# RWKV attention and two MoE layers: most tiles' keys and outputs are turned through DRAM, and the second MoE's row fetches change places with its weights

## The chip, the cores and the metric

One core of one Trainium2 chip runs the kernel. The metric is device time in microseconds (us). Before the change, three runs took 840.63, 841.93 and 843.02 us, a median of 841.93.

## The reference

Three layers follow one another, in fp32. B = 4 batches, H = 8 heads, S = 768 steps, D = 48.

```python
for t in range(S):                               # attention, state is 48 x 48 per head
    cur = einsum('bhd,bhe->bhde', u[None] * k[t], v[t])
    y[t] = einsum('bhd,bhde->bhe', r[t], state + cur)
    state = w[t][..., None] * state + einsum('bhd,bhe->bhde', k[t], v[t])
x = y as (B*S = 3072 tokens, H*D = 384)
xn = x / sqrt(mean(x*x) + 1e-6) * rms_g          # MoE 1: gated, 384 -> 1536 -> 384
x = (silu(xn @ w_gate) * (xn @ w_val)) @ w_out
e = argmax(x @ w_gate2)                          # MoE 2: the best of 8 experts, 384 -> 1024 -> 384
out = prob[e] * sigmoid(x @ w_output_gate)[e] * (relu(x @ w1[e]) @ w2[e])
```

## The kernel before

**Attention in tiles.** The recurrence is worked in 24 tiles, each of 128 steps of one batch (six chunks of four batches). A tile is a generator, `attention` (L384), in steps that end at each `yield`. In each step of 128 tokens the keys and receptances are scaled by running products of the decay. A tile's 8 heads lie as four pairs (`NPR`): `kq`, the scaled keys, is 128 partitions (channels of a pair) by 4 x 128 tokens. The steps are: the backward scan (L404, VectorE); `kq` (L422); the forward scan `rq`, its product and the bonus reduction (L430, L433, L440); the decay of the state; the scores on TensorE and their masking to `am` (L530, L538, VectorE); the turning of `kq` into tokens x channels (`kt`: four TensorE transposes, L469, and a copy by ACT, L471; they precede the scores); the values (L563) and key times value (`sp`, L552), the sum `y` (L572), its mean square (ACT, POOL); the state's update (L588); the scaling of `y` (L596, ACT); and the turning of `y` into channels x tokens (three TensorE transposes, L600), from which `xh` (ACT, L604) and `xl` (VectorE, L607) are split: each product of MoE 1 and MoE 2 is three passes, high x high, high x low, low x high (`mm3`, all at L191).

The last chunk's four tiles (20 to 23) need no `kt`, because no state follows.

**MoE 1 in stages.** Eight stages, j = 0 to 7, hold 384 tokens (three tiles) each. TensorE works first-layer products (`l1`, two halves a block f: gate and value) and second-layer ones (`l2`) for 12 blocks f; ACT makes `sil`, VectorE the product (`sil`, L670), ACT `hh` (L672), VectorE `hl` (L675). In stage j the attention of the three tiles of stage j + 1 is worked between them.

**Who sets the order.** Each engine runs its own queue in program order. `Plan` (L772) is a table of slots: a stage has one slot after the first half of `l1`, one after `hh` and one after `l2`, 36 in all, and a tile's step number k is written at slot a * TGAP + OFFS[k], for its tile a = 0, 1, 2 of the stage. Before, TGAP is 9 and OFFS is (0, 2, 4, 6, 8, 10, 11, 13, 15). SP's queue issues nearly all DMAs, in program order; a DMA whose source is not ready holds those behind it.

**MoE 2 in units.** Rows of each expert were scattered to DRAM (`scr`). Unit 0 is 256 rows of the largest expert, unit 1 its other 272; units 2 to 8 are experts 1 to 7, 448 to 352 rows. A unit is `l1` in KF2 = 8 blocks f (plus two for `l2`); in it the next unit's rows are turned (`turn_next`, L759) and split, and the next expert's weights are fetched (`raw`, L178 and L165; three 384 KB buffers in flight in MoE 1's last stages, four later), and split by ACT (L160) and VectorE (L161). The rows of a unit are fetched by `gather` (four DMAs into `z`, L751, and one into `xg`, L1095). Before, unit 0 fetches unit 1's rows at f = 2, loads the ids of all seven other experts to SP at f = 4 (L1406), and fetches unit 2's rows at f = 6; expert 1's weights come in unit 1, and unit 1 fetches unit 3's rows at f = 5.

Of the kernel before, what the change touches and what calls it, by code (L numbers as in the profile page):

```python
# [9 lines left out]
F32 = mybir.dt.float32  # L10
# [12 lines left out]
def kernel(  # L23
# [17 lines left out]
    TURN_AT=2,  # L41
# [15 lines left out]
    DSLOT=(1, 2),  # L57
    OFF0=((0, 2.0, 6.2, 8.5, 8.5, 11.0, 12.5, 12.5, 15.2), (9.4, 11.9, 14.1, 16.9, 17.2, 19.9, 19.9, 21.8, 23.3), (17.8, 19.3, 24.0, 26.0, 26.8, 27.8, 30.3, 30.8, 30.8)),
    OFFS=(0, 2, 4, 6, 8, 10, 11, 13, 15),
    TGAP=9.0,  # L60
    START_SEQ=(-1, -6, -3, -6, 99, -12, 0, 0, -6, 0, 1, 1, 0, -1, 0, 1, -6, 1, 0, 9, -5, 0, 2, 1, 0, 9, 2, -1, 0, -5, 1, 2, 1, 9, 1, -7, 2, 2, 9, 2, 9, -2, 1, 2, 2, 9, -6, -6, -1, 2),
):
    nc = tc.nc
# [4 lines left out]
    P = 128  # L68
# [311 lines left out]
            )  # L380

    START = START_SEQ

    def attention(c, i, xh, xl, col):  # L384

# [34 lines left out]
        front = c["front"].rearrange("p (a t) -> p a t", t=SEG)  # L420
        nc.vector.reciprocal(front[:, :, 0:1], decay)
        nc.vector.tensor_tensor(out=kq, in0=kT, in1=kq, op=ALU.mult)  # L422
        kt_mul = nc.vector if i in KT_DVE else nc.gpsimd
        if bare and i not in KT_DVE:
            kt_mul.tensor_tensor(out=kT, in0=kT, in1=rT, op=ALU.mult)
# [172 lines left out]
        xT = bank("m", 3, [P, KD, P])  # L598
        for kk in range(KD):
            nc.tensor.transpose(xT[:, kk], y2[:, kk * P:(kk + 1) * P], c["ident"])  # L600
        cs = slice(col, col + P)
        for kk in range(KD):
            gk = c["g"][:, kk:kk + 1]
# [198 lines left out]
    with tc.manual_schedule():  # L802
# [184 lines left out]
        for j in range(NB):  # L987
# [24 lines left out]
            for f in range(KF + 2):  # L1012
                if f < KF:
                    if j == 0:
                        weights_to(f + f // 2 + 1)
                    hs[f] = l1(f, xs[0], xs[1], n, slot, j == 0 and f // 2 < WHOLE)
                if f >= 2:
                    if (f - 2) // 2 in routed:
                        exhaust(routed.pop((f - 2) // 2))
                    if j == 0 and (f - 2) // 2 < WHOLE:  # L1020
                        l2_whole(f - 2, hs.pop(f - 2), acc)
                    else:
                        if (f - 2) // 2 not in wo:
                            split_wo((f - 2) // 2)
                        l2(f - 2, hs.pop(f - 2), acc)
                    slot()
                if j == NB - 1:
                    if f == 3:
                        lead = pick(c)
                        xw = expert_weights(0, lead)  # L1030
                    if f >= 4:
                        next(xw, None)
                    if f == KF - 3:
                        both = ring_view([2, EARLY * KD])
                        z0 = both[:, 0].rearrange("p (j c) -> p j c", c=DQ)
                        xT0 = both[:, 1].rearrange("p (k t) -> p k t", k=KD)
                        early = scr.rearrange("(e a) c -> e a c", e=E)[ds(lead, 1)]
                        load_blocks(z0, early, 0, EARLY // 32)
                        xg0 = late.tile([P, EARLY // P, ROW - DM], F32, name="xg0")
                        nc.sync.dma_start(  # L1040
                            out=xg0,
                            in_=early[:, 0:EARLY, DM:ROW].rearrange("o (t p) c -> p (o t) c", p=P),
                        )
                    if f == KF:
                        x0 = ring_view([2, KD, EARLY], FR)
                        for kk in range(KD):
                            turn(z0, xT0, kk)
                        for kk in range(KD):
                            split_in(xT0, EARLY, x0[:, 0], x0[:, 1], kk)
                if j == 1:  # L1050
                    for e in INIT_AT.get(f, ()):
                        init_rows(c, e)
            plan.finish()
            if j == 0:
                decs.close()
                late = ctx.enter_context(
                    tc.tile_pool(name="late", bufs=1, side="right", reuse_waits="tile")
                )
                route_constants(c, late)
                pr = ph1.enter_context(tc.tile_pool(name="pr", bufs=1, reuse_waits="tile"))  # L1060
            if j == NB - 2:
                rawp = ph1.enter_context(tc.tile_pool(name="rawp", bufs=3, reuse_waits="tile"))
            if j + 1 < NB:
                xr = pr.tile([P, nt, WIDTH], F32, tag="xr", name="xr")
# [252 lines left out]
        xg_cur, x_cur = xg0, (x0[:, 0], x0[:, 1])  # L1317
        for ui, (k, r0, n) in enumerate(units):
            last_of = ui + 1 == NU or units[ui + 1][0] != k
            if ui and last_of:  # L1320
                nxw = expert_weights(k + 1, expert[k + 1]) if k + 1 < E else iter(())
            xh, xl = x_cur
            a, b2 = ew[k]
# [9 lines left out]
            if ui == 0:  # L1333
                plan.add(
                    route(c, starts[NB - 1], sizes[NB - 1], xr, True), 0,
                    ROUTE_AT,
                )

            def gather_unit(i):
# [20 lines left out]
            for f in range(KF2 + 2):  # L1360
                if f < KF2:
# [13 lines left out]
                if ui and f == GATHER_AT and ui + 2 < NU:  # L1375
                    gathered[ui + 2] = gather_unit(ui + 2)
                if ui + 1 < NU:
                    if ui and f >= TURN_AT:
                        next(turns, None)
                    if not ui and f == KF2:  # L1380
                        exhaust(turns)
# [16 lines left out]
                    plan.step()  # L1398
                if ui == 0 and f == 2:
                    gathered[1] = gather_unit(1)  # L1400
                if ui == 0 and f == KF2 - 2:
                    gathered[2] = gather_unit(2)
                if ui == 0 and f == 4:
                    ids = order()
                    expert += [
                        nc.values_load(  # L1406
                            ids[0:1, q:q + 1], engines=(mybir.EngineType.SP,), min_val=0,
                            max_val=E - 1,
                        )
                        for q in range(E - 1)  # L1410
                    ]
            exhaust(post)
            if by_row:
                for i, o in enumerate(acc):
# [78 lines left out]
```

## Time and profile before

| | |
|---|---|
| median of three runs | 841.93 us |
| profiled execution | 841.91 us, span 840.2 us |
| TensorE (PE) busy | 811.9 us, 97% |
| weight loads (PEld) | 763.7 us, 91% |
| VectorE (DVE) | 536.5 us, 64% |
| ScalarE (ACT) | 327.3 us, 39% |
| GpSimd (POOL) | 199.5 us, 24% |
| TensorE clock granted, mean | 0.99 of full speed |
| DMA | 88.97 MB, 106 GB/s over the span |

Idle time that the profile names "idle before" is that of the engine of the row, and the arrow names what ended it. A timeline row with x3 is three like instructions joined, and its duration runs from the first start to the last end; TensorE's matmuls overlap, so that what one costs is read from the next one's start, not from its duration.

### The profile page before, as it was taken

The numbers are of one execution on the slowest core, as the hardware profiler recorded it, in microseconds if no ns is written. First come the engines' busy times: TensorE is split into PE (matmuls) and PEld (weight loads), VectorE is DVE, ScalarE is ACT, GpSimd is POOL, SyncE is SP. The second block draws the span as 40 slices with busy tenths as digits, with TensorE's granted clock in tenths as the row PEclk, the third lists the DMA queues.
The fourth block names the chain that finished last, engine by engine and source line by source line (L and its number), as shares of the span: only waits on it lengthen the run. The fifth ranks groups of instructions, "written<-read, shape, count | busy, mean of one in ns | idle before, by whom it ended". The sixth has DMA issues, their size and how long they took to land. (4 is left out here: it accounts for less than half of the span.)

```text
span 840.2 us, 19796 instructions
## 1 busy us (share of the span) xinstructions
PE 811.9 (97%) x8007; PEld 763.7 (91%) x8007; DVE 536.5 (64%) x1155; ACT 327.3 (39%) x718; POOL 199.5 (24%) x286
## 2 busy tenths in 40 slices
PE   8799999999999999999999999999979999999995
PEld 5588789999999999999999999999879999999994
DVE  8788857755774774685575476334747686677751
ACT  6756543233323233223323322323425434454430
POOL 4544523213321231132131131010101022112111
PEclk9899999999999999999999999999999999999998
DMA  8955527561320240222122020023167655565410
GB/s 214 286 162 161 151 59 211 139 150 48 104 70 11 58 121 24 55 90 58 48 87 68 25 81 2 2 86 95 54 165 189 170 124 159 155 177 154 153 44 24
DMA packets 78500, 88.97 MB, mean 106 GB/s; under 512 B 23345, under 2 KB 69847, under 8 KB 78407
## 3 DMA queue, kind: packets, MB, share of 16 engines
q1 hardware_dynamic: 74768, 78.10, 34.6%
q0 software_dynamic: 3312, 9.56, 3.1%
q8 instruction: 63, 1.03, 0.5%
q14 instruction: 31, 0.25, 0.1%
q10 hardware_dynamic: 326, 0.03, 0.0%
HBM read 71.25 MB, written 16.78 MB: 105 GB/s over the span
## 5 line engine op out<-in xcount | busy, mean ns | idle before, releaser
L191 PE MATMUL a<-xh,gv 128*128 128x384 f32 x1152 | 317.8, 342 | 1.4 <-ACT xh L604 1.4
L191 PEld LDWEIGHTS a<-xh,gv 128*128 128x128 f32 x1152 | 210.8, 188 | 4.0 <-ACT xh L604 1.6
L191 PE MATMUL a<-xl,gv 128*128 128x384 f32 x576 | 194.3, 337 | 0.5 <-DVE xl L607 0.5
L191 PE MATMUL l<-wo,hh 128*128 128x400 f32 x504 | 134.6, 348 | 0.0
L670 DVE TENSOR_TENSOR sil<-a,sil 128x384 f32<-128x384 f32 x84 | 46.7, 556 | 108.3 <-PE a L191 106.5
L191 PE MATMUL a<-xh,w1s 128*128 128x272 f32 (+7 forms) x384 | 107.9, 342 | 4.5 <-DVE hl L1142 4.5
L191 PEld LDWEIGHTS a<-xl,gv 128*128 128x128 f32 x576 | 108.6, 189 | 1.2 <-DVE xl L607 0.7
L663 ACT ACTIVATE sil<-a 128x384 f32<-128x384 f32 x96 | 47.2, 492 | 156.1 <-PE a L191 155.6
L672 ACT ACTIVATE hh<-sil 128x384 fp32r<-128x384 f32 x84 | 44.1, 525 | 133.3 <-DVE sil L670 133.3
L191 PEld LDWEIGHTS l<-wo,hh 128*128 128x128 f32 x504 | 90.8, 188 | 1.0
L191 PE MATMUL l<-wo,hl 128*128 128x400 f32 x252 | 86.5, 343 | 0.0
L278 POOL DMA_INDIRECT out_dram<-row,iu x30 | 35.3, 1178 | 188.9 <-DVE row L1153 164.7
L1142 DVE SCALAR_TENSOR_TENSOR hl<-a,hh 128x256 fp32r<-128x256 f32 (+8 forms) x72 | 38.6, 539 | 62.6 <-ACT hh L1141 62.4
L191 PEld LDWEIGHTS a<-xh,w1s 128*128 128x128 f32 x384 | 71.3, 192 | 5.9 <-DVE hl L1142 4.7
L675 DVE TENSOR_TENSOR hl<-sil,hh 128x384 fp32r<-128x384 f32 x84 | 55.7, 663 | 30.2 <-ACT hh L672 29.6
L1141 ACT ACTIVATE hh<-a 128x256 fp32r<-128x256 f32 (+8 forms) x72 | 34.3, 476 | 98.1 <-PE a L191 96.4
L191 PE MATMUL l<-hh,rows 128*128 128x272 f32 (+4 forms) x240 | 67.9, 347 | 0.0
L191 PE MATMUL a<-xl,w1s 128*128 128x272 f32 (+7 forms) x192 | 65.5, 341 | 0.2 <-DVE xl L764 0.2
L191 PEld LDWEIGHTS l<-wo,hl 128*128 128x128 f32 x252 | 47.2, 188 | 0.0
L191 PEld LDWEIGHTS l<-hh,rows 128*128 128x128 f32 x240 | 44.6, 191 | 1.0
L191 PE MATMUL l<-rows,hh 128*128 128x384 f32 (+2 forms) x176 | 45.2, 338 | 0.0
L453 POOL TENSOR_TENSOR y<-vt,g 128x384 f32<-128x384 f32 x18 | 15.1, 837 | 123.5 <-issue 85.8
(259 smaller groups left out, 1335.3 us busy)
## 6 DMA issues: line engine op xcount, KB each, us to landing
raw<-in_moe_w_dram SPq DMA_DIRECT2D x64, 384.0 KB, 3.9
set<-in_feat_dram SPq DMA_DIRECT2D x46, 192.0 KB, 3.7
rk<-in_rkv_dram SPq DMA_DIRECT2D x19, 384.0 KB, 4.1
scr<-zrow SPq DMA_DIRECT2D x8, 788.0 KB, 7.3
set<-in_feat_dram SPq DMA_DIRECT2D x46, 96.0 KB, 2.5
vt<-in_rkv_dram SPq DMA_DIRECT2D x23, 192.0 KB, 3.1
raw<-in_moe_w_gate_dram SPq DMA_DIRECT2D x8, 384.0 KB, 4.7
raw<-in_moe_w_val_dram SPq DMA_DIRECT2D x8, 384.0 KB, 5.8
```

Of the source, the lines that this page charges most:

```text
L191: nc.tensor.matmul(o, a, b, start=start and i == 0, stop=stop and i == 2, skip_group_check=True)
L278: ins = nc.gpsimd.indirect_dma_start(out=dst, out_offset=bass.IndirectOffsetOnAxis(ap=idx, axis=0), in_=rows, in_offset=None, bounds_check ...
L453: nc.gpsimd.tensor_tensor(out=y, in0=vv, in1=g.unsqueeze(2).to_broadcast([P, H, D]), op=ALU.mult)
L663: nc.scalar.activation(out=sil, in_=o, func=AF.Silu)
L670: nc.vector.tensor_tensor(out=sil, in0=pg[1], in1=sil, op=ALU.mult)
L672: nc.scalar.activation(out=hh, in_=sil, func=AF.Copy)
L675: nc.vector.tensor_tensor(out=hl, in0=sil, in1=hh.bitcast(F32), op=ALU.subtract)
L1141: nc.scalar.activation(out=hh, in_=o, func=AF.Relu)
L1142: nc.vector.scalar_tensor_tensor(out=hl, in0=o, scalar=0.0, in1=hh.bitcast(F32), op0=ALU.max, op1=ALU.subtract)
```

## The change

From tile 9 on (`BLOCKS`), `kq` (except in the last chunk: 11 tiles) and the scaled `y` (15 tiles) are written to a scratch in DRAM by one DMA, and read back by four, each for 32 partitions in pieces of 32 x 4 bytes, so that each 32 x 32 square lands in the place that it has in the turned matrix. One VectorE instruction then turns every square (L567 and L626 of after). The 89 TensorE transposes (44 and 45) and ACT's copies to `kt` of these tiles go. `xh` and `xl` read the turned `y` from SBUF. The tiles of these stages get other slots.

```diff
+    OFFB=(0, 0, 1, 3, 10, 11, 12, 13, 14, 19),
+    TGAPB=8.0,
+    BLOCKS=9,
...
+    def through(place, t, how, z):
+        nc.sync.dma_start(out=place, in_=t)
+        src = place.rearrange(how, i=4, j=4, r=32, c=32)
+        a = z.shape[1] // P
+        for i in range(4):
+            q = z[32 * i:32 * i + 32].rearrange("p (a j c) -> p a j c", a=a, j=4)
+            nc.sync.dma_start(out=q, in_=src[i])
...
+        by_blocks = i >= BLOCKS
+        if not last and by_blocks:
+            kt_z = blk.tile([P, NPR * P], F32, tag="kz", name="kz")
+            through(kd[i % 2], kq, "(j r) a (i c) -> i r a j c", kt_z)
...
-        if not last:
+        if not last and not by_blocks:
             kt_ps = bank("m", 3, [P, NPR, P])
...
+        if by_blocks:
+            if not last:
+                kt = p1.tile([P, NPR, P], F32, tag="kt", name="kt")
+                nc.vector.transpose(out=kt.rearrange("p a t -> p (a t)"), in_=kt_z)
+            yield
...
         nc.scalar.activation(out=y2, in_=y2, func=AF.Copy, scale=ss)
+        if by_blocks:
+            y_z = blk.tile([P, DM], F32, tag="yz", name="yz")
+            through(yd[i % 2], y2, "(j r) (k i c) -> i r k j c", y_z)
+        yield
+        if by_blocks:
+            xT = blk.tile([P, KD, P], F32, tag="yt", name="yt")
+            nc.vector.transpose(out=xT.rearrange("p k t -> p (k t)"), in_=y_z)
...
-                        a * TGAP if j else 0, OFFS if j else OFF0[a],
+                        a * (TGAPB if j > 1 else TGAP) if j else 0,
+                        OFFB if j > 1 else OFFS if j else OFF0[a],
...
-                    if f == KF:
+                    if f == KF - 1:
                         x0 = ring_view([2, KD, EARLY], FR)
...
-            if ui and last_of:
+            if ui > 1 and last_of:
                 nxw = expert_weights(k + 1, expert[k + 1]) if k + 1 < E else iter(())
...
-                next(nxw, None)
+                if ui or f in (KF2 - 2, KF2 - 1):
+                    next(nxw, None)
...
+                if ui == 1 and f == 2:
+                    gathered[2] = gather_unit(2)
+                if ui == 1 and f == KF2 + 1:
+                    next_expert()
+                if ui == 2 and f == 0:
+                    gathered[3] = gather_unit(3)
...
-                    if ui and f >= TURN_AT:
+                    if ui > 1 and f >= TURN_AT + (2 if ui == 2 else 0) or ui == 1 and f >= TURN_AT + 3:
                         next(turns, None)
...
-                if ui == 0 and f == KF2 - 2:
-                    gathered[2] = gather_unit(2)
                 if ui == 0 and f == 4:
                     ids = order()
-                    expert += [
...
+                    next_expert()
+                    nxw = expert_weights(1, expert[1])
```

(`next_expert` loads one id to SP's registers; the next ids are loaded just before each later unit's gather.) Of TensorE's queue only the transposes and the places of the attention's steps change; VectorE's and SP's queues show the rest.

VectorE before, in a stage, from a tile's forward scan (`rq`) to its scores' masks (`am`); `xl` between them belongs to the tile ahead of it, and `sil` and `hl` to MoE 1:

```order
L430 SCALAR_TENSOR_TENSOR rq<-set_81,front 128x516
L433 TENSOR_TENSOR rq<-set_81,rq 128x4x128
L440 TENSOR_REDUCE g<-rk 128x8
L670 TENSOR_TENSOR sil<-a,sil 128x384
L675 TENSOR_TENSOR hl<-sil,hh 128x384
L607 SCALAR_TENSOR_TENSOR xl<-m,g_col,xh 128x128 x3
L490 TENSOR_TENSOR states<-states,kq 128x192
L670 TENSOR_TENSOR sil<-a,sil 128x384
L530 TENSOR_TENSOR am_84<-a,tri_83 128x4x64
L538 TENSOR_TENSOR am_84<-a,tri_83 64x2x64 x2
L530 TENSOR_TENSOR am_85<-m,tri_83 128x4x64
L538 TENSOR_TENSOR am_85<-m,tri_83 64x2x64 x2
```

VectorE now, at the like place in a stage from j = 2 on; the scan is the third tile's, `am` and `kt` are the second tile's, `yt` and `xl` the first tile's:

```order
L448 SCALAR_TENSOR_TENSOR rq<-set_81,front 128x516
L451 TENSOR_TENSOR rq<-set_81,rq 128x4x128
L458 TENSOR_REDUCE g<-rk 128x8
L705 TENSOR_TENSOR hl<-sil,hh 128x384
L548 TENSOR_TENSOR am_84<-a,tri_83 128x4x64
L556 TENSOR_TENSOR am_84<-a,tri_83 64x2x64 x2
L548 TENSOR_TENSOR am_85<-m,tri_83 128x4x64
L556 TENSOR_TENSOR am_85<-m,tri_83 64x2x64 x2
L626 STREAM_TRANSPOSE yt<-yz 128x384
L637 SCALAR_TENSOR_TENSOR xl<-yt,g_col,xh 128x128 x3
L567 STREAM_TRANSPOSE kt<-kz 128x512
```

The third tile's scan now stands ahead of the second tile's masks, and between these and the turning of the second tile's keys (L567, which its key times value needs) lie the first tile's `yt` and `xl`.

SP before, in MoE 2's unit 0, from the last fetch for unit 1 (`xg`, 16 x 10) through the ids of the experts to the fetch of unit 2's rows (`z`, 14 pieces) and expert 1's first weights (`raw`):

```order
L1100 DMA xg<-scr 16x10
L1406 TENSOR_LOAD order
L1406 ISA x2
...
L751 DMA z<-scr 32x14x96
...
L1095 DMA xg<-scr 128x4x10
L178 DMA raw<-in_moe_w_dram 128x3x256
L165 DMA raw<-in_moe_w_dram 128x2x384
```

SP now, at the like place:

```order
L1134 DMA xg<-scr 16x10
L1376 TENSOR_LOAD order
L1376 ISA x2
L181 DMA raw<-in_moe_w_dram 128x3x256
L168 DMA raw<-in_moe_w_dram 128x2x384
...
L181 DMA raw<-in_moe_w_dram 128x3x256
L781 DMA z<-scr 32x14x96
...
L1129 DMA xg<-scr 128x4x10
L168 DMA raw<-in_moe_w_dram 128x2x384
```

One id is loaded in place of seven, and five weight fetches now stand ahead of unit 2's rows.

## Rows read from the trace of the kernel before

**Rows 1.** Windows: microseconds; busy (instructions) per engine; clock; DMA share; GB/s

```profile
334.70:402.90 68.20, 68.20 (x831) 65.85 (x830) 43.09 (x100) 21.71 (x52) 16.15 (x24) 1.00 0.23 63
```

**Rows 2.** Timeline of PE: start, microseconds, line, operation, tile; stage j=3

```profile
361.89 0.52 PE L191 MATMUL l<-wo,hh 128*128 128x400 f32 x2
...
363.52 0.49 PE L600 MATMUL m<-ident,y 128*128 128x128 f32 x3
363.84 0.60 PE L469 MATMUL m<-ident,kq 128*128 128x128 f32 x4
364.20 0.42 PE L191 MATMUL a<-xh,gv 128*128 128x384 f32 x1
364.46 0.34 PE L191 MATMUL a<-xl,gv 128*128 128x384 f32 x1
...
367.23 0.34 PE L191 MATMUL a<-xh,gv 128*128 128x384 f32 x1
...
368.78 0.63 PE L191 MATMUL l<-wo,hh 128*128 128x400 f32 x2
```

**Rows 3.** Timeline of PE: values, key times value, stage j=2

```profile
321.86 0.38 PE L563 MATMUL m<-vt,am 128*32 128x48 f32 x16
...
322.56 0.52 PE L552 MATMUL m<-vt,kt 128*32 128x48 f32 x32
```

**Rows 4.** VectorE by form: count, busy, mean ns, idle before

```profile
L759 DVE STREAM_TRANSPOSE xT<-z 128x384 f32<-128x384 f32 x6 | 4.1, 687 | 0.0
L607 DVE SCALAR_TENSOR_TENSOR xl<-m,g_col,xh 128x128 fp32r<-128x128 f32 x72 | 20.8, 345 | 16.7 <-ACT xh L604 16.6
```

**Rows 5.** Timeline of VectorE: one tile among stage j=3

```profile
360.89 1.22 DVE L430 TENSOR_TENSOR_SCAN rq<-set,front 128x516 f32<-128x516 f32 x1
...
363.26 0.54 DVE L670 TENSOR_TENSOR sil<-a,sil 128x384 f32<-128x384 f32 x1
...
368.47 0.42 DVE L530 TENSOR_TENSOR am<-a,tri 128x256 f32<-128x256 f32 x1 [0.23 <-PE m L523]
...
370.39 0.56 DVE L675 TENSOR_TENSOR hl<-sil,hh 128x384 fp32r<-128x384 f32 x1
```

**Rows 6.** DMA issues: tile, queue, count, KB each, median landing time

```profile
vt<-in_rkv_dram SPq DMA_DIRECT2D x23, 192.0 KB, 3.1
z<-scr SPq DMA_DIRECT2D x8, 168.0 KB, 5.3
...
xg<-scr SPq DMA_DIRECT2D x3, 15.0 KB, 2.0
```

**Rows 7.** Timeline of ACT: end of stage j=2

```profile
325.54 0.53 ACT L672 ACTIVATE hh<-sil 128x384 fp32r<-128x384 f32 x1 [1.18 <-DVE sil L670]
...
328.46 0.61 ACT L596 ACTIVATE y<-y,ss 128x384 f32<-128x384 f32 x1
```

**Rows 8.** Timeline of PE: first matmul of stage j=3

```profile
334.66 0.33 PE L191 MATMUL a<-xh,gv 128*128 128x384 f32 x1
```

**Rows 9.** Windows: ends of MoE1 and of the first expert

```profile
594.00:596.00 2.00, 0.99 (x5) 0.47 (x4) 2.00 (x6) 1.34 (x4) 0.00 (x0) 1.00 0.00 0
627.83:633.83 6.00, 6.00 (x27) 6.00 (x28) 5.40 (x17) 1.80 (x5) 0.00 (x0) 0.52 0.97 218
634.00:636.00 2.00, 2.00 (x18) 2.00 (x17) 2.00 (x4) 1.60 (x3) 0.00 (x0) 1.00 0.89 122
```

**Rows 10.** Timeline of ACT: first expert

```profile
617.75 0.40 ACT L1141 ACTIVATE hh<-a 128x272 fp32r<-128x272 f32 x1 [0.90 <-PE a L191]
624.93 0.84 ACT L160 ACTIVATE w1s<-raw 128x768 fp32r<-128x768 f32 x1 [6.78 <-DMA raw<-in_moe_w_dram]
```

**Rows 11.** Timeline of PE: the first matmul after the wait

```profile
627.83 0.59 PE L191 MATMUL a<-xh,w1s 128*128 128x272 f32 x1 [4.48 <-DVE hl L1142]
```

**Rows 12.** SP queue: start, issue time, transfer

```profile
610.57 0.33 SPq L1100 DMA_DIRECT2D xg<-scr  x1
615.14 1.90 SPq L751 DMA_DIRECT2D z<-scr  x4
```

More of the change, by code (lines that the diff above doesn't have):

```diff
@@ L382 @@
     START = START_SEQ
+    kd = [dram.tile([P, NPR, P], F32, name=f"kd{i}") for i in range(2)]
+    yd = [dram.tile([P, DM], F32, name=f"yd{i}") for i in range(2)]
+    def through(place, t, how, z):
[5 more added lines that the diff above has]
+            nc.sync.dma_start(out=q, in_=src[i])
     def attention(c, i, xh, xl, col):
@@ L596, in attention @@
         nc.scalar.activation(out=y2, in_=y2, func=AF.Copy, scale=ss)
+        if by_blocks:
+            y_z = blk.tile([P, DM], F32, tag="yz", name="yz")
+            through(yd[i % 2], y2, "(j r) (k i c) -> i r k j c", y_z)
         yield
-        xT = bank("m", 3, [P, KD, P])
-        for kk in range(KD):
-            nc.tensor.transpose(xT[:, kk], y2[:, kk * P:(kk + 1) * P], c["ident"])
+        if by_blocks:
+            xT = blk.tile([P, KD, P], F32, tag="yt", name="yt")
+            nc.vector.transpose(out=xT.rearrange("p k t -> p (k t)"), in_=y_z)
+        else:
+            xT = bank("m", 3, [P, KD, P])
+            for kk in range(KD):
+                nc.tensor.transpose(xT[:, kk], y2[:, kk * P:(kk + 1) * P], c["ident"])
         cs = slice(col, col + P)
@@ L1060 @@
                 pr = ph1.enter_context(tc.tile_pool(name="pr", bufs=1, reuse_waits="tile"))
+                blks = ph1.enter_context(ExitStack())
+                blk = blks.enter_context(tc.tile_pool(name="blk", bufs=2, reuse_waits="tile"))
             if j == NB - 2:
+                blks.close()
                 rawp = ph1.enter_context(tc.tile_pool(name="rawp", bufs=3, reuse_waits="tile"))
@@ L1336, with next_expert @@
                     ROUTE_AT,
+                )
+            def next_expert():
+                q = len(expert) - 1
+                expert.append(
+                    nc.values_load(
+                        ids[0:1, q:q + 1], engines=(mybir.EngineType.SP,), min_val=0,
+                        max_val=E - 1,
+                    )
                 )
@@ L1371 @@
                         next(post, None)
-                next(nxw, None)
+                if ui or f in (KF2 - 2, KF2 - 1):
+                    next(nxw, None)
                 if ui >= 3:
                     next(listing, None)
-                if ui and f == GATHER_AT and ui + 2 < NU:
+                if ui == 1 and f == 2:
[4 more added lines that the diff above has]
+                    gathered[3] = gather_unit(3)
+                if ui > 1 and f == GATHER_AT and ui + 2 < NU:
+                    next_expert()
                     gathered[ui + 2] = gather_unit(ui + 2)
                 if ui + 1 < NU:
-                    if ui and f >= TURN_AT:
+                    if ui > 1 and f >= TURN_AT + (2 if ui == 2 else 0) or ui == 1 and f >= TURN_AT + 3:
                         next(turns, None)
@@ L1400 @@
                     gathered[1] = gather_unit(1)
-                if ui == 0 and f == KF2 - 2:
-                    gathered[2] = gather_unit(2)
                 if ui == 0 and f == 4:
                     ids = order()
-                    expert += [
[L1406 to L1411, printed above, removed]
+                    next_expert()
+                    nxw = expert_weights(1, expert[1])
             exhaust(post)
```

## Prediction

> **What bounds the kernel now.** I read the page's busy shares first, then the slices, then windows of single stages, then TensorE's idle time by what ended it. TensorE bounds MoE 1: in stage j = 3, 68.20 us long, it is busy for all 68.20, at clock 1.00, while VectorE works 43.09, ACT 21.71 and DMA has a share of 0.23 [rows 1]. So work taken from TensorE there is worth its full length, and work added elsewhere costs only where TensorE comes to wait for it. Outside the stages TensorE idles in two places that the change touches: between 594 and 596 us it works 0.99 of 2.00 [rows 9], and in the first expert of MoE 2 one matmul stands behind 4.48 us of idle time [rows 11], after which the granted clock is 0.52 for six microseconds [rows 9].
>
> **Transposes that go.** Three of y and four of kq stand between an l2 and an l1: the first starts at 363.52, the first l1 matmul behind them at 364.20, 0.68 later; that matmul's successor comes 0.26 later instead of the usual 0.17 [rows 2]. I charge the extra 0.085 to them: 0.765 us for seven, 0.109 each. Eighty-nine go: 9.7 us. By stage: 21 of them in j = 2, 3 and 4 (2.3 us each), 17 in j = 5 (1.85; tile 20 has no kt), 9 in j = 6 (0.98). ACT loses its copies to kt as well, which were hidden.
>
> **New work on VectorE.** The trace has this square-wise turning for 128x384: 0.687 us [rows 4]. In proportion 128x512 takes 0.92. A stage gets 3 x (0.69 + 0.92) = 4.8 us more; 43.1 + 4.8 is far under 68.2, so VectorE doesn't become the bound. But it works in order, and the new order puts the third tile's scan, product and reduction, the second tile's masks and the first tile's yt and xl ahead of the second tile's kt, for which its key times value waits two slots behind the scores. I walk both queues from the end of the l1 half before the scores. VectorE: sil 0.48, the scan and what follows it 2.37 (360.89 to 363.26), hl 0.5, masks 1.92 (368.47 to 370.39) [rows 5], yt 0.69, ACT's xh 0.35 (as one xl), three xl 0.9 [rows 4], kt 0.92: 8.1 us. TensorE: l2 1.63 (361.89 to 363.52), scores with the old state's part 1.38 (to 368.78), two l1 halves of 1.56 (nine spacings of 0.17) [rows 2], values 0.70 [rows 3]: 6.8. TensorE waits 1.3 us. For the third tile, counted from the end of the scores: VectorE 1.6 (to the masks' end, 368.78 to 370.39) + 0.5 + 0.69 + 0.35 + 0.9 + 0.92 = 5.0, TensorE 1.63 + 1.56 + 0.70 = 3.9: 1.1 us. The first has no such neighbours: 0.1. So 2.5 us a stage come back in j = 2 to 4, 1.4 in j = 5 and none in j = 6. From below the wait may be nothing, if sil or the masks start earlier than in the walk; from above, one more hl (0.5) ahead of each makes 3.5.
>
> **The way through DRAM.** No row shows a write and four reads of 128-byte pieces. For the write I take 2.7 us, between xg's 2.0 and vt's 3.1 (192 KB, as y is); for the issues of the second to fourth read 1.4 (four z issues take 1.90 [rows 12]); for the last read's landing 2.2, near xg's 2.0 (15 KB in pieces of 40 bytes) and under z's 5.3 (168 KB each) [rows 6]. That makes r = 6.3 us; the ends are 5.5 (2.0 + 1.4 + 2.0) and 9.8 (3.1 + 1.4 + 5.3). Keys have ten slots for it, and hide it. The first two tiles' y has five slots (some 9.5 us). The third tile's y has to reach the next stage's first matmul. In stage j = 2, hh of block 10 ends at 326.07 and the scaling, now a slot earlier, takes 0.61 [rows 7]: 326.7. With r, yt 0.69, xh and the first xl 0.35 each the operands are there at 334.4, and that matmul starts at 334.66 before [rows 8], less some 0.3 that the stage has been shortened: a wait of about 0.1 to 0.4, taken 0.4, at each of five boundaries (into j = 3 to 7). There every us that r is above 6.3 costs 5 us in all; beyond some 7.2 the yt of the earlier tiles also holds up VectorE's queue ahead of kt, for 4 us more per us (one in each of j = 2 to 5). SP gets five issues a transfer and waits for the write in between; behind it stand vt and sets for later tiles, which are fetched a tile (some 15 us) ahead, so I cost that at nothing; without this lead a late vt would stop the values.
>
> The Trainium skill, page "DMA: Bandwidth & Descriptors", section "Specifications", gives 512 bytes as the least transfer for line rate, and a read-modify-write below it. That speaks against these 128-byte pieces. The nearest row, xg's 384 pieces of 40 bytes in 2.0 us [rows 6], does not show it; it holds 15 KB where a square read holds 48 or 64.
>
> **Sum of MoE 1.** j = 2 to 4: 3 x (-2.3 + 2.5 + 0.4) = 1.8; j = 5: -1.85 + 1.4 + 0.4 = -0.05; j = 6: -0.98 + 0.4 = -0.6. Together +1.2 us: what the transposes give, VectorE's waits take back.
>
> **MoE 2.** In the 4.48 us, TensorE waits for hl, hl for hh on ACT, and ACT stands in order behind a weight split whose raw landed only at 624.93, 6.78 us after ACT's last work [rows 10]. SP explains the lateness: between the last small fetch (610.57 + 0.33) and the next one (615.14) it loads seven ids, 4.2 us, and then issues unit 2's rows ahead of the first weight [rows 12]. Now one id is loaded (a seventh of 4.2, 0.6) and the first weight leaves near 611.6, where before it stood behind fetches that began at 615.14 and took two more us to issue; so it lands before ACT comes to its split. The stall goes: -4.5. With no idle time ahead of it I let the clock stay up: the six us at 0.52 hold 27 matmuls, where two us at full clock hold 18 of the same kind or near it, so up to 3.0 us; since the counts mix sizes I take 2.3. What is late next is unit 2's rows: the fifth weight waits for a free buffer, that is for the first one's landing (four to six us after 611.6) and split, until some 617.8, so z leaves at 618.3 to 621 and lands near 624 to 625, for turns that start with f = 5 of unit 1; the last split, now behind the copies of the outputs, costs 0.5 at the next boundary (0 to 1.1). The earlier turn for unit 0 takes the 1.0 us of 594 to 596. Sum: -4.5 - 2.3 - 1.0 + 0.5 = -7.3.
>
> Together +1.2 - 7.3 = -6.1. The profiled execution took 841.91 us (span 840.2), as the median of 841.93; **835.8 us**.
>
> **Rivals.**
> (1) The squares come late. For it: four reads of small pieces each behind a write, and z's 5.3 us. Against: xg. At r = 8.1 it costs 1.8 x 5 + 0.9 x 4 = 12.6 more: 848.4 us. It decides for slower (above 844.4) from r = 7.7.
> (2) VectorE's waits don't show and the stages' ends neither, since VectorE idles a third of each stage and slots can drift: all 9.7 us count, and 841.9 - 9.7 - 7.3 = 824.9.
> (3) MoE 2's stall moves instead of going: unit 2's rows, behind five weights and a buffer's release, come as late as the weights did, and TensorE waits at unit 2 with the low clock behind it. For it: the DMA share there was 0.97 [rows 9]. Then only the 1.0 remains: 841.9 + 1.2 - 1.0 = 842.1.
>
> **How the numbers follow.** Forecast 0.48, with a range of its own of 831 to 840 (waits of 1 to 3.5 a stage, the clock's part 1 to 3); late squares 0.22; no waits 0.13; moved stall 0.17. A measurement can tell 0.3%, 2.5 us, from no change: faster is under 839.4, slower over 844.4. The forecast gives 0.44 of faster and 0.04 of same, no waits 0.13 of faster, the moved stall 0.16 of same and 0.01 of slower, late squares 0.02 of same and 0.20 of slower: faster 0.57, same 0.22, slower 0.21. The range of 827 to 846 leaves out most of the late squares, whose upper end (r = 9.8) would be near 864, and half of "no waits".
>
> **What would show it.** Stages j = 2 to 4 of about 68 us, with TensorE waits for kt on VectorE of 1.1 to 1.3 us ahead of key times value, some seven in all, and under 0.5 us for xl or xh at each stage's start; squares that return in about 6 us from the scaling's end; in the first expert no idle time of TensorE over 1 us and a clock of 1.00. Wrong: waits of over 1.5 us at the stages' starts (rival 1), stages of 66 us (rival 2), a wait of several us for z or its turn at unit 2 (rival 3).

## The result

The changed kernel takes 845.89 us (median of six, 843.94 to 848.09) against 841.45 us before: a ratio of 1.0057, with a 95% interval from 1.0038 to 1.0077. It is slower; 835.8 us was forecast. From one trace to the other, stages 2 to 6 of MoE 1 went from 338.5 to 346.6 us (+8.1; forecast +1.2), and MoE 2's first three units with the stage ahead of them from 133.5 to 128.4 (-5.1; forecast -7.3). Three single executions of 1086 to 2781 us, one of them of the kernel before, are left out of the ratios in this document.

Stages are counted here as the code counts them, j = 0 to 7. The rows, and the prediction where it reads them, give two stages of the trace before as j = 2 and j = 3 that are 3 and 4 by this count (the window of [rows 1] is stage 4). The prediction's sum goes by the right count and does not change.

Two windows of the changed kernel: stage j = 4 and a stretch in stage 3 (columns as in [rows 1]; the engines are PE, PEld, DVE, ACT and POOL).

```profile
340.22:410.26 70.04, 66.88 (x810) 64.10 (x810) 46.64 (x106) 19.90 (x49) 17.99 (x24) 1.00 0.40 100
327.58:330.99 3.41, 3.41 (x12) 3.40 (x12) 0.52 (x2) 0.63 (x3) 2.52 (x3) 0.50 0.23 62
```

Where TensorE was busy for the whole of a stage, it now idles 3.2 of 70.04 us, with 21 fewer matmuls. What it waited for in stages 2 to 5 (us in total, times, longest), in the changed kernel:

```profile
PE m L575 <- DVE kt L567: 6.8, 7, 1.8
PE m L575 <- DVE t L766: 3.7, 4, 0.9
PE m L758 <- DVE am L556: 1.7, 3, 0.7
PE a L194 <- DVE am L556: 0.8, 1, 0.8
```

Eleven waits stand ahead of key times value, four ahead of the routing's ranks and an l1 product; there was none of these before. Idle time is not all of it. TensorE's timeline at the first tile of stage 4:

```profile
363.21 0.19 PE L758 MATMUL m<-oh,tri 128*128 128x24 bf16 x1 [0.70 <-DVE am L556]
...
363.93 0.35 PE L586 MATMUL m<-turned_v,am 128*32 128x48 f32 x16
365.22 0.54 PE L575 MATMUL m<-vt,kt 128*32 128x48 f32 x32 [0.93 <-DVE t L766]
```

From the start of the values' last group (363.93) to that of key times value it takes 1.29 us; before, four such groups take 0.70, 0.17 each [rows 3]. So a wait that is shown as 0.93 costs 1.12. VectorE at that time:

```profile
362.58 0.58 DVE L556 TENSOR_TENSOR am<-m,tri 64x128 f32<-64x128 f32 x2
...
363.66 0.70 DVE L567 STREAM_TRANSPOSE kt<-kz 128x512 f32<-128x512 f32 x1
...
364.99 0.17 DVE L766 TENSOR_TENSOR t<-m,base 128x24 f32<-128x24 f32 x1
```

The masks end at 363.16, after which the ranks' product (L758) can have its bank; then come kt and, 0.6 us after its end, the reading of the ranks (`t`), to which the trace puts down the wait of key times value. VectorE's busy time in that stage, in windows of 3 us (length, busy, clock, DMA share, GB/s):

```profile
355.00:358.00 3.00, 2.97 (x5) 1.00 0.00 0
358.00:361.00 3.00, 2.97 (x4) 1.00 0.29 87
361.00:364.00 3.00, 2.93 (x9) 1.00 0.42 66
...
373.00:376.00 3.00, 2.97 (x5) 1.00 0.20 34
376.00:379.00 3.00, 2.96 (x8) 1.00 0.52 125
...
385.00:388.00 3.00, 0.24 (x1) 1.00 0.94 235
```

For nine us, and again for six, VectorE has next to no room; some ten us after the second stretch it is nearly idle. Over the whole stage it is busy 46.64 of 70.04, which is what the prediction looked at. Before the change, a window of 3 us can be as full, but the ones beside it are not (stage 5):

```profile
442.00:445.00 3.00, 1.42 (x6) 1.00 0.25 71
445.00:448.00 3.00, 2.96 (x6) 1.00 0.00 0
448.00:451.00 3.00, 1.57 (x3) 1.00 0.82 205
```

**The way through DRAM.** The transfers of y, its writes and its reads (count, KB each, median us to landing):

```profile
yd<-y SPq DMA_DIRECT2D x15, 192.0 KB, 2.0
yz<-yd SPq DMA_DIRECT2D x60, 48.0 KB, 2.4
```

ACT's scaling of y for a second tile (stage 3) and a third tile (stage 4), and VectorE's turning of each:

```profile
313.59 0.61 ACT L619 ACTIVATE y<-y,ss 128x384 f32<-128x384 f32 x1
...
401.89 0.60 ACT L619 ACTIVATE y<-y,ss 128x384 f32<-128x384 f32 x1
```

```profile
324.10 0.58 DVE L626 STREAM_TRANSPOSE yt<-yz 128x384 f32<-128x384 f32 x1 [1.23 <-DMA yz<-yd]
...
408.74 0.58 DVE L626 STREAM_TRANSPOSE yt<-yz 128x384 f32<-128x384 f32 x1 [1.40 <-DMA yz<-yd]
```

The third tile's y is back 408.74 - 402.50 = 6.2 us after its scaling's end; at the other four boundaries it is 6.3 to 6.6. That is r as forecast, and TensorE waits at none of the boundaries. Each read of 48 KB in pieces of 128 bytes lands in 2.4 us, the write of 192 KB in 2.0. The pieces are under the 512 bytes that the Trainium skill gives as the least for line rate ("DMA: Bandwidth & Descriptors", section "Specifications"). What that costs is not shown, as no run here reads the same squares in longer pieces. But the second tile's y in stage 3 took 9.9 us. SP's queue:

```profile
310.44 1.79 SPq L358 DMA_DIRECT2D set<-in_feat_dram  x2
...
314.23 0.37 SPq L391 DMA_DIRECT2D yd<-y  x1
319.17 2.57 SPq L396 DMA_DIRECT2D yz<-yd  x4
```

Its write was issued at once, right behind the loads for a later tile, and the reads, which wait for it, only 4.9 us later. In stages 2 and 4, where the second tile's write left 0.9 and 1.4 us after such loads, its reads followed after 3.6 and 3.2 us, and where no loads stood ahead (the third tiles), after 1.9. The third tile's key times value then waited 1.84 us, the longest of all, and the clock stood at 0.50 for 3.41 us after it (the second window above), some 1.7 us more.

**MoE 2.** The stall of 4.48 us [rows 11] and the half clock behind it [rows 9] are gone. ACT's splits of weights in unit 1, and TensorE's longest wait there:

```profile
624.11 0.83 ACT L163 ACTIVATE w1s<-raw 128x768 fp32r<-128x768 f32 x1
...
635.90 0.84 ACT L163 ACTIVATE rows<-raw 128x768 fp32r<-128x768 f32 x1 [2.08 <-DMA raw<-in_moe_w_dram]
```

```profile
641.62 0.39 PE L194 MATMUL l<-hl,rows 128*128 128x272 f32 x1 [1.32 <-DVE hl L1176]
```

The first split finds its weight there. A later one, whose fetch stands behind unit 2's rows on SP, waits 2.08 us, and TensorE 1.32 some five us later, when the splits behind it had held up hl. Unit 1 as a whole went from 26.1 to 20.7 us, unit 2 from 30.4 to 30.9; from stage 7's start to unit 1's it is 77.0 before and 76.9 after, because the waits at unit 0's start, 1.0 us before, are gone, and one of 0.9 for hl has come there.

### The profile page after: what moved, and what is told of

It reads as the page before. It is cut to its first block, busy times and chain, and to the rows that moved or that the text cites. A ratio compares the mean times of both kernels' runs of the same rounds, so it can differ in the third digit from the quotient of the medians.

```text
span 843.8 us, 19831 instructions
## 1 busy us (share of the span) xinstructions
PE 805.2 (95%) x7918; PEld 755.2 (89%) x7918; DVE 554.1 (66%) x1181; ACT 321.8 (38%) x707; POOL 209.9 (25%) x286
## 5 line engine op out<-in xcount | busy, mean ns | idle before, releaser
L194 PE MATMUL a<-xh,w1s 128*128 128x272 f32 (+7 forms) x384 | 106.2, 337 | 0.0
L705 DVE TENSOR_TENSOR hl<-sil,hh 128x384 fp32r<-128x384 f32 x84 | 51.8, 617 | 25.4 <-ACT hh L702 24.8
L604 POOL TENSOR_TENSOR ss<-ss,mhalf 128x1 f32<-128x1 f32 x24 | 16.4, 683 | 131.2 <-ACT ss L601 131.0
L471 POOL TENSOR_TENSOR y<-vt,g 128x384 f32<-128x384 f32 x18 | 17.1, 948 | 115.5 <-DVE g L458 100.8
```

Source lines behind the costliest of these rows:

```text
L194: nc.tensor.matmul(o, a, b, start=start and i == 0, stop=stop and i == 2, skip_group_check=True)
L471: nc.gpsimd.tensor_tensor(out=y, in0=vv, in1=g.unsqueeze(2).to_broadcast([P, H, D]), op=ALU.mult)
L604: nc.gpsimd.tensor_tensor(out=ss, in0=ss, in1=c["mhalf"], op=ALU.pow)
L705: nc.vector.tensor_tensor(out=hl, in0=sil, in1=hh.bitcast(F32), op=ALU.subtract)
```

## The experiments

Times are medians; each ratio is to the kernel before on the same chip (840.4 to 841.8 us).

**The parts by themselves.** One kernel has only the edits around MoE 2, one only the turning and the slots.

```diff
-    OFFB=(0, 0, 1, 3, 10, 11, 12, 13, 14, 19),   TGAPB=8.0,   BLOCKS=9,
+    OFFB=(0, 2, 4, 6, 8, 10, 11, 13, 15),        TGAPB=9.0,   BLOCKS=24,
```

> Only the changes around MoE 2 (order of fetches, ids one by one, the earlier turn for its first unit); every tile is turned on TensorE in the old slots. Between the two traces MoE 2 and the stage before it took 5.1 us less with the change. If that part stands by itself, as I think: 841.5 - 5.1 = 836.4 us (835.5 to 837.5). If the gain hangs on the new attention before it (other timing of SP and ACT): over 839.

839.01 us, 0.9978 (0.9960 to 0.9996): a gain of some 2 us, not 5. In its trace unit 1 holds waits of 1.68 and 1.34 us for splits that wait for weights. The attention's stages are as before (338.5 us). The forecast is missed; 839 was its bound for a gain that hangs on the attention ahead.

The other leaves the lines of MoE 2 as they were before:

```diff
-                if ui == 1 and f == 2:
-                    gathered[2] = gather_unit(2)
...
+                if ui == 0 and f == KF2 - 2:
+                    gathered[2] = gather_unit(2)
```

> Only the way through DRAM and the new slots from tile 9 on; MoE 2 as before. Stages 2 to 6 took 8.1 us longer in the changed kernel's trace. If the parts add up: 841.5 + 8.5 = 850 us (848 to 852), the stall of 4.5 us in MoE 2's first expert back. If the loss came from the two parts together: under 846.

848.48 us, 1.0076 (1.0050 to 1.0102). By the medians the parts add up, within a microsecond: +7.3 and -2.2 for a measured +4.4. In this run's trace the first three units of MoE 2 with the stage ahead take 131.7 us, 1.8 less than before, though their lines are those of before; with the 3.5 us of the run with the fetches alone that makes about the changed kernel's 5.1. By these traces, part of what MoE 2 gained there came from the attention ahead of it; how is left open.

**kt earlier on VectorE.**

```diff
-    OFFB=(0, 0, 1, 3, 10, 11, 12, 13, 14, 19),   # kt behind the masks
+    OFFB=(0, 0, 1, 3, 8, 10, 12, 13, 14, 19),    # kt ahead of the scores
```

> The changed kernel, with each tile's kt turned on VectorE at slot 8 after the tile's start, ahead of the next tile's scans and of its own scores, not behind the masks and the former tile's yt and xl. Theory A (what stands ahead of kt in VectorE's queue makes TensorE wait): the eleven waits ahead of key times value (10.5 us idle, 12.5 with what restarting costs) and the half clock of 3.4 us in stage 3 go, 1 or 2 us come back as waits for the masks: 845.9 - 12.5 - 1.7 + 1.5 = 833 us (831 to 836). Theory B (the squares return late, or the DRAM traffic slows the stages): waits stay, now for the DMA of kz ahead of kt: over 843.

838.81 us, 0.9974 (0.9958 to 0.9990): 7 us less than the changed kernel. Theory B falls; theory A's 831 to 836 is missed too. In the trace stages 2 to 6 take 338.4 us, 8.2 less, but MoE 2's first units with the stage ahead 130.9, which is 2.5 more, with a new half clock of 3.41 us in unit 1. TensorE's waits in stages 2 to 5 of this run:

```profile
PE m L574 <- DVE t L765: 3.0, 4, 0.8
PE m L757 <- DVE am L561: 1.9, 4, 0.6
PE a L194 <- DVE am L561: 1.3, 2, 1.1
```

The waits for kt are gone, and so is the half clock in stage 3. What stays are the ranks and the masks of the first tile.

**The slots without the squares.**

```diff
-    OFFB=(0, 0, 1, 3, 10, 11, 12, 13, 14, 19),   BLOCKS=9,
+    OFFB=(0, 0, 1, 6, 10, 12, 13, 14, 19),       BLOCKS=24,
```

> The changed kernel with every tile turned on TensorE again, but in the new slots (tiles 8 slots apart, scans at 0, 0, 1, scores at 10, values at 12, y turned at 19; kt's transposes at 6). Theory A says that the next tile's scans ahead of the masks cost by themselves, less than with kt and yt on VectorE: 1 to 4 us over the run with the fetches alone, 837.5 to 840.5. If the slots alone are at fault: 8 us over it, 844. If the turning alone is at fault: the same as it, 836.4.

854.17 us, 1.0152 (1.0134 to 1.0169), worse than any forecast. In these slots the y transposes wait for the second tile's masks on VectorE (6.0 us over five stages) and the next stage for xh and xl (two waits of 0.46 at each boundary). The slots belong to the squares, and the kernel is no clean test of the slots alone; but VectorE is late in it too, without any squares to turn.

**The routing's ranks moved.** On the run with keys early, and on the changed kernel:

```diff
-    ROUTED=((29, 30), (6, 12), (2, 6)),
+    ROUTED=((29, 30), (6, 15), (2, 6)),
```

> The run with keys early, and the second step of MoE 2's routing (the ranks, a TensorE product into a PSUM bank that VectorE then reads) at slot 15 of a stage, not at slot 12 with the first tile's values. In the trace with keys early TensorE still waits in each of stages 2 to 5 some 0.5 us for the masks ahead of that product and 0.76 us for VectorE's reading of the ranks ahead of the first tile's key times value. Theory A2 (the first tile's wait is for the bank that the ranks hold, not for its kt): both go, with restarts 1.6 us a stage in four stages: 838.8 - 6.4 = 832.5 us (831 to 834.5). Theory A as predicted it at first (kt and masks alone): the waits come back with kt or the masks as their cause, 837 or more.

> The changed kernel with only the routing's second step moved to slot 15. By A2 the first tile's waits (0.93 us idle, 1.1 with the restart, in four stages) and the masks' (0.3 to 0.7 in three) go, those of the second and third tiles for kt stay: 845.9 - 6.5 = 839.5 us (838 to 842). If the first tile's wait is for kt: no less than 844.

842.70 us (1.0019, 0.9999 to 1.0038) and 848.99 us (1.0100, 1.0066 to 1.0134): both missed, and by much. The waits for the ranks are gone in both, and others came. The two runs' largest:

```profile
PE a L194 <- DVE am L561: 8.8, 5, 1.9
```

```profile
PE m L575 <- DVE kt L567: 7.9, 11, 1.0
PE a L194 <- DVE am L556: 6.8, 5, 1.4
```

With kt early, TensorE now waits up to 1.9 us for the second tile's masks, five times; without, the first tile waits for its kt after all (eleven waits for kt, where there were seven). The bank was where the lateness showed, not what made it: a wait that is taken away shows at the next thing that VectorE owes.

**The work spread.**

```diff
-    OFFB=(0, 0, 1, 3, 8, 10, 12, 13, 14, 19),
+    OFFB=(0, 1, 3, 5, 8, 10, 12, 13, 14, 19),
```

> As the run with the routing later, and the next tile's two scans spread: first steps at 0, 1, 3, 5 of a tile, not 0, 0, 1, 3, so that a tile's forward scan, product and reduction (2.4 us of VectorE) stand behind the masks of the tile ahead of it. If these scans hold up the masks of the second tile (waits of up to 1.06 us for the bank that the masks read, in stage 5): 1 to 3 us less than with the routing later, 830.5 us. If not: the same within 1 us.

834.94 us, 0.9913 (0.9884 to 0.9942), faster than both kernels; against the run with the routing later, 842.70, it is 8 us (1 to 3 were expected). Only the places of the scans, the keys and the decay changed, and the waits for masks, kt and ranks are gone, so the work that stood ahead of these was their cause. Late squares weren't: VectorE waits longer for them here than with the routing later (23.4 us against 7.4). Nor is it enough that VectorE is full: from 413.88 to 425.70 in stage 5 it works without a pause, for 11.8 us (12.7 is the longest such stretch in the changed kernel, 6.6 before), and TensorE doesn't wait there. But in that stretch the masks now stand ahead of the forward scan:

```profile
418.74 0.41 DVE L553 TENSOR_TENSOR am<-a,tri 128x256 f32<-128x256 f32 x1
...
421.13 1.23 DVE L448 TENSOR_TENSOR_SCAN rq<-set,front 128x516 f32<-128x516 f32 x1
```

What is left in stages 2 to 6, TensorE's longest wait and VectorE's wait for squares:

```profile
PE a L194 <- DVE sil L699: 3.8, 3, 1.9
```

```profile
DVE yt L625 <- DMA yz<-yd: 23.4, 13, 3.3
```

**Old spacing, new collision.**

```diff
-    OFFB=(0, 0, 1, 3, 10, 11, 12, 13, 14, 19),   TGAPB=8.0,
+    OFFB=(0, 2, 4, 6, 8, 8, 10, 11, 12, 17),     TGAPB=9.0,   # kt ahead of the scores
```

> The changed kernel (squares through DRAM, its MoE 2) with the tiles 9 slots apart again and a tile's steps at 0, 2, 4, 6 (scans, keys, decay), kt turned at 8 ahead of the scores at 8, values at 10, state at 11, y scaled at 12 and turned at 17. Theory C (in the new slots VectorE has full stretches of 9 to 12 us, at 2.97 of 3 us busy, in each of which TensorE waits wherever it meets VectorE; taking one wait away only shows it the next): with the work spread as before, VectorE keeps up, the waits of stages 2 to 5 go, and the 9.3 us that the transposes took are left over: 839 (fetches alone) - 9.3 + up to 2 for stage boundaries = 830.5 us (829 to 833). If VectorE's 4.8 us more a stage can't be hidden wherever it stands: waits of 1 to 2 us a stage stay, 836 to 840.

> The slots of the run with the old spacing, and MoE 2 as in the run with ids alone (rows stay ahead of the weights; no earlier turn for its first unit). If both gains are real and lie in different places they add: 837.2 - 9.3 + up to 2 = 828.5 us (826 to 831). If the fetches' order only matters with the attention of before: as the old spacing, 830 or more.

879.50 us (1.0456, 1.0436 to 1.0476) and 877.93 us (1.0446, 1.0424 to 1.0468): a miss of 49 us. ACT, SP and VectorE at a first tile's y in the run with the old spacing:

```profile
222.69 0.60 ACT L618 ACTIVATE y<-y,ss 128x384 f32<-128x384 f32 x1
```

```profile
223.68 0.56 SPq L391 DMA_DIRECT2D kd<-kq  x1
226.34 2.69 SPq L396 DMA_DIRECT2D kz<-kd  x4
229.12 0.58 SPq L391 DMA_DIRECT2D yd<-y  x1
232.51 2.56 SPq L396 DMA_DIRECT2D yz<-yd  x4
```

```profile
237.05 0.58 DVE L625 STREAM_TRANSPOSE yt<-yz 128x384 f32<-128x384 f32 x1 [5.04 <-DMA yz<-yd]
```

The y is scaled by 223.29, but the second tile's keys went to SP just ahead of it: their reads wait for their own write, and the write of y, queued behind them, leaves at 229.12. The square is back 13.8 us after the scaling; VectorE stands in order at its turning, and TensorE at the masks, 35.4 us in all, with seven stretches at half clock. Squares that come late are what the first rival foresaw, but not for its reason: here one trip holds up another on SP's queue, and the pieces have no part in it that is shown.

```diff
-    OFFB=(0, 2, 4, 6, 8, 8, 10, 11, 12, 17),
+    OFFB=(0, 2, 4, 6, 8, 8, 10, 11, 13, 17),
```

> As the run with the old spacing, with the scaling of y one slot (some 1.9 us) later, at 13; the turning stays at 17. The prediction has it that the third tile's y has no slack at the five stage boundaries (in the changed kernel the squares came back 6.3 us after the scaling's end, VectorE waiting 1.1 to 1.7 us for them, TensorE not): then each of five boundaries costs up to 1.9 us, 5 to 9.5 us over the old spacing. If there is slack: the same within 1 us.

899.40 us (1.0704, 1.0667 to 1.0742), 20 us over the old spacing. TensorE's new wait:

```profile
PE a L194 <- ACT xh L633: 10.6, 5, 2.5
```

Five boundaries wait 1.9 to 2.5 us each, as the prediction's price for late squares there says (no slack, 1.9 us a slot). Behind four of them the clock stands at 0.50 for 3.41 us, and with the longer stretches elsewhere the half clock costs some 8.5 us more than with the old spacing, most of the rest.

In the next, the keys set out behind the y:

```diff
-    OFFB=(0, 2, 4, 6, 8, 8, 10, 11, 12, 17),
+    OFFB=(0, 4, 5, 6, 8, 10, 10, 11, 12, 17),    # kt behind the scores again
...                                               # MoE 2 as with the ids alone
```

> Tiles 9 slots apart as in the run with the old spacing, but a tile's keys at 4, not 2, so that they set out on SP behind the y of the tile ahead (at 12), not right ahead of it; steps 0, 4, 5, 6, scores 8, kt 10, values 10, then 11, 12, 17; MoE 2 as with ids alone. In the run with the old spacing a y scaled at 223.3 us had its write issued at 229.1 behind the keys' reads, and came back 13.6 us after its scaling; VectorE waited 5.0 us and TensorE 3.8 to 5.3 us, twice a stage. Theory F (the order of the two trips on SP's queue did that): these 35 us go, and 837.2 - 9.3 + up to 4 = 830 us (827 to 833). If tiles 9 slots apart can't hold the trips: 845 or more.

856.18 us (1.0170, 1.0136 to 1.0203): 22 us less than the 877.93 of the run with the old spacing and the same MoE 2, but the loss is not all gone, and the forecast is missed. VectorE's waits for squares in stages 2 to 5:

```profile
DVE yt L626 <- DMA yz<-yd: 11.1, 8, 1.9
DVE kt L567 <- DMA kz<-kd: 8.3, 5, 3.9
```

Now the keys come late, behind the y. Whichever goes first, tiles 9 slots apart with these steps leave the other trip behind it too little time.

And the run with the scans spread, with a slot more for the squares:

```diff
-    OFFB=(0, 1, 3, 5, 8, 10, 12, 13, 14, 19),   TGAPB=8.0,
+    OFFB=(0, 1, 3, 5, 8, 10, 12, 13, 14, 20),   TGAPB=7.5,
...                                              # MoE 2 as with the ids alone
```

> The slots of the run with the scans spread, tiles 7.5 slots apart, not 8, and y turned at 20, not 19: one slot (1.9 us) more between a y's scaling and its turning; MoE 2 as in the run with ids alone. In the run with the scans spread VectorE waits up to 3.3 us for yz, and TensorE then 0.7 to 1.9 us for VectorE's sil, once a stage. Theory F (what is left there comes from squares that return late behind the keys' trip and the loads on SP's queue): these waits go, 3 to 6 us less than the same without the slack: 827 us (825 to 829). If the waits come from VectorE's fullness: they stay or grow with tiles closer together, 831 or more.

835.19 us, 0.9923 (0.9895 to 0.9951); missed by 8 us. VectorE's waits for yz fall from 23.4 to 8.0 us:

```profile
DVE yt L625 <- DMA yz<-yd: 8.0, 6, 1.7
```

so most of the lateness is gone, and TensorE's waits for sil with it, but the tiles closer together brought seven waits of some 0.4 us and one of 1.16 ahead of the old state's products (4.1 us in all; the profile names no cause). The like kernel without the slack is the last one below, with runs from 831.2 to 838.7 us: no gain is shown.

**MoE 2 taken apart.** The ids one by one, and nothing else:

```diff
-                    expert += [nc.values_load(ids[0:1, q:q + 1], ...) for q in range(E - 1)]
+                    next_expert()          # and once ahead of each later unit's rows
```

> The kernel before with one edit: the experts' ids are loaded one by one, each ahead of its unit's fetch, not seven at once; weights and rows keep their order. If the seven loads (4.2 us) made the first expert's weights late, as the prediction has it: they come 3.6 us earlier, the stall of 4.5 us goes to about 1 and the half clock goes: 841.2 - 5.5 = 835.5 us (834 to 837.5). If what bounds is the amount that SP has to fetch there (672 KB of rows and 3 MB of weights in one unit), the wait comes back at a later weight: 839 to 841 us.

837.18 us, 0.9948 (0.9929 to 0.9967), inside the forecast's range: a gain of 4.4 us, where all the MoE 2 edits together gave 2. Unit 1 takes 19.6 us, not 26.1. The first three units with the stage ahead of them take 127.0 to 127.4 us in this trace and in the four others with this MoE 2, and 128.3 to 130.9 in the nine with the changed kernel's.

```diff
-                if ui == 1 and f == 2:
-                    gathered[2] = gather_unit(2)
...
+                    gathered[2] = gather_unit(2)      # unit 0, f = 4, ahead of the weights
                     nxw = expert_weights(1, expert[1])
```

> The run with the fetches alone, with one edit: the rows of unit 2 are fetched in unit 0 right behind the first id, ahead of the five weight fetches, and turned from f = 2 of unit 1; the weights still start in unit 0. In the traces with the rows behind the weights ACT waits up to 2.7 us for the raw weights behind these rows, and TensorE 1.2 to 1.7 us twice. Theory D (the rows among the weights make the later weights late, while the ids' early end already cures the first ones): as with ids alone, 837.2 (836 to 838.5). If the weights' early start is what matters and the rows' place does not: 839.0 as with the fetches alone.

840.80 us, 1.0006 (0.9992 to 1.0019): no gain, theory D falls. ACT in the run with ids alone, then ACT and TensorE in this one:

```profile
617.89 0.40 ACT L1141 ACTIVATE hh<-a 128x272 fp32r<-128x272 f32 x1 [0.90 <-ACT hh L1141]
619.81 0.84 ACT L160 ACTIVATE w1s<-raw 128x768 fp32r<-128x768 f32 x1 [1.52 <-DMA raw<-in_moe_w_dram]
```

```profile
619.49 0.84 ACT L163 ACTIVATE w1s<-raw 128x768 fp32r<-128x768 f32 x1 [3.63 <-DMA raw<-in_moe_w_dram]
```

```profile
621.73 0.40 PE L194 MATMUL a<-xh,w1s 128*128 128x272 f32 x1 [2.82 <-DVE hl L1176]
```

The first weight is used at the same time in both, but here ACT has come to it two hh sooner, and stands there for 3.63 us with those hh behind it.

```diff
-                if ui or f in (KF2 - 2, KF2 - 1):
+                if ui > 1 or ui == 1 and f >= 2 or not ui and f in (KF2 - 2, KF2 - 1):
```

> The run with the rows first, with expert 1's first weight splits two blocks later in unit 1 (behind three of ACT's hh, not one), as they stand in the run with ids alone; SP's order of fetches is nearly the same in all three. Theory G (ACT, in order, stands at a split whose weight lands at 619.5 to 619.8 us in both traces; what decides is how many hh stand ahead of it): the wait of 2.8 us goes, 837.2 as with ids alone (836 to 838.5). If the weights' time of arrival decides: 840.8 as with the rows first.

835.79 us, 0.9929 (0.9905 to 0.9953). The first split, at the same time, after 1.24 us:

```profile
619.86 0.84 ACT L163 ACTIVATE w1s<-raw 128x768 fp32r<-128x768 f32 x1 [1.24 <-DMA raw<-in_moe_w_dram]
```

With only the splits' place in ACT's and VectorE's queues changed, and SP's fetches in the same order, 5 us are gained: theory G holds.

At last, both gains in one kernel:

```diff
-    OFFB=(0, 0, 1, 3, 10, 11, 12, 13, 14, 19),
+    OFFB=(0, 1, 3, 5, 8, 10, 12, 13, 14, 19),    # kt ahead of the scores, ranks at 15
...
+                    next_expert()                # MoE 2 as with the ids alone
```

> The attention of the run with the scans spread (834.9 us) and MoE 2 as in the run with ids alone. In the traces MoE 2 with the stage before it took 130.7 us in the one and 127.0 in the other: 834.9 - 3.7 = 831.2 us (830 to 833). If MoE 2's gain depends on the attention's timing: 834 or more.

The ratio is 0.9901 (0.9867 to 0.9935), with three runs at 831.2 to 831.8 us, as expected, and three at 836.2 to 838.7. The profiled one, at 838.69, has two waits of over 2.1 us in the attention for sil behind late squares, each followed by a stretch of half clock; whether the low three have none was not profiled. The gains add, if at all, only in those.

## Why the prediction was wrong

- **The step that failed most** is "far under 68.2, so VectorE doesn't become the bound", with the walk behind it. The average over the stage hid stretches in which VectorE is full, and the walk asked what stands ahead of kt for two tiles only. For these it was right: second tile 1.3 us forecast, 0.97 measured, and the two turnings, 0.33 us shorter than assumed, would make up the difference; third tile 1.1 forecast, 0.52 measured, and once 1.84. But "The first has no such neighbours: 0.1" was wrong: the second tile's scans and keys stand right ahead of the first tile's masks, and the routing's ranks behind these. It waited 0.93 us in each of four stages, and the masks held up the ranks or an l1 product for another 2.5 us in all. The run with the scans spread, in which the forward scans stand behind the masks, has none of these waits.
- **Left out of the sum:** what a wait costs beside its idle time. Of the +8.1 us, idle waits are 13.0 (3.7 first tiles, 3.9 second, 2.9 third, 2.5 masks; 8.9 forecast), the half clock 1.7; the transposes give an estimated 8.4, by stage 6, where 9 went with hardly a wait (66.01 to 65.16 us, 0.094 each, 0.109 forecast). What is left, some 1.8 us, would be restarts behind fifteen waits, 0.12 each, where the one looked at took 0.19.
- **Boundaries:** right about r and about the lack of slack (the run with y later), too high by 0.4 us each. That r came out is partly luck: at the end of stage 4 the write took 1.9 us, not 2.7, the issues 1.9, not 1.4, and the last landing 2.4, not 2.2.
- **"so I cost that at nothing"** for SP's loads looked at the loads' lateness, not at what they do to a write behind them: 9.9 us, once, and the longest wait. In the run with the scans spread each of TensorE's three waits for sil (3.8 us in all) comes behind a square whose write left right behind such loads; its reads followed 4.5 to 5.5 us later. In the run with the old spacing it is the keys' trip, not loads, that stands ahead of the write, and TensorE waits 35.4 us.
- **MoE 2:** the stall's cause was named rightly (seven ids: the run with ids alone gains 4.4 us by its ratio) and so was its half clock. "it lands before ACT comes to its split" was right of the first weight; wrong was to leave the later ones at 0.5 us: the edit moved the splits up in ACT's queue by two blocks, and put rows among the fetches. The rows, which the prediction expected late, cost TensorE at most 0.2 us; the weights behind them came late. What the ids' end gave, these took back in part, 1.4 us in the changed kernel's trace and 3.0 in that of the fetches alone (MoE 2 with the stage ahead of it is 6.6 us shorter with the ids alone, 5.1 and 3.5 in these). The 1.0 us at unit 0's start was not gained either.
- **The rivals.** None is right as written: late squares (0.22) gave the sign, but r stayed at 6.3 us and the boundaries did not wait; the stall that moves (0.17) was half true, with a part of it moving to later weights. That 845.89 us lies just inside the range of 827 to 846 is luck, because that end of the range stood for late squares.

## What to carry to other kernels

Before calling an engine off the bound, read its busy time in windows as short as the gap between two of its deadlines, in the new order: here a share of two thirds over a stage held stretches of nine us without room. Then ask, for everything that the bounding engine needs out of such a stretch, what stands ahead of it, for every tile and not only for the one whose order changed most. A wait taken away can come back at the next thing owed; moving the work that stands ahead is what helped here. And an in-order queue that carries a write and the reads that wait for it is taken until those reads are issued: in the run with the old spacing the keys' trip held SP for 5.4 us, and the y behind it left 5.8 us late.

## What was not expected of the hardware

- A TensorE wait of 0.93 us costs 1.12 from start to start. Nearly all its waits of over 2 us in these traces (32 of 34, from 190 to 700 us) came with a stretch at a granted clock of 0.50, mostly of 3.4 or 6.8 us; one of 1.84 us did, too.
- Reads of 48 KB in 128-byte pieces landed in 2.4 us each, a plain write of four times their size in 2.0.
- VectorE turned 128x512 in 0.70 us and 128x384 in 0.58, less than the 0.92 and 0.69 forecast.
